# Batch 1's attention by pairs of heads: 64-row score products of two heads, and one split of q and k for each pair

## The chip, the cores and the metric

The kernel runs on one core of a Trainium2 chip. The metric is device time in microseconds (us) of one execution, the median of three runs. TensorE multiplies matrices, VectorE (DVE), ScalarE (ACT) and GpSimd (POOL) work on tiles in the on-chip memory, and DMA queues, most of them fed by SyncE (SP), carry data. An operand of TensorE has up to 128 rows; a product over 64 rows uses the lower or the upper half of them. One operand (the weights) is loaded by an instruction of its own, shown as PEld.

## The reference

Attention of two batches with eight heads each, 768 positions, 64 numbers a head. A query sees only the keys that fall into the same of 64 buckets. The result goes through two blocks of matrix products. The parts that this case touches are the scores:

```python
q_bits = (np.einsum('bhsd,dk->bhsk', q, proj) > 0)      # 6 bits
q_bucket = np.sum(q_bits * 2 ** np.arange(6), axis=-1)  # k the same
mask = q_bucket[:, :, :, None] == k_bucket[:, :, None, :]
scores = scale * np.matmul(q, k.transpose(0, 1, 3, 2))
scores = np.where(mask, scores, -1e9)
attn = np.exp(scores - max);  attn = attn / (sum + 1e-9)
x = np.matmul(attn, v)                    # then, per batch:
u = x + real(fft(fft(x, 1), 2));  un = layernorm(u)
x = u + relu(un @ w_ch1) @ w_ch2          # 512 -> 2048 -> 512
theta = x @ w_theta;  y = w_tok_r @ (x * cos) + w_tok_i @ (x * sin)
out = (x + y) + relu((x + y) @ w_ch)
```

All weights arrive as float64 and are split in the kernel into parts of which TensorE computes three products.

## The kernel before

**Stages.** Batch 0's attention runs first. Its Fourier products, layer norm and first block follow. Batch 1's attention is woven into that: its softmax work runs on VectorE, ScalarE and GpSimd while TensorE also works on batch 0's Fourier products and its two-layer MLP (names psm, unT, w1h, w1l, hh). Batch 1's Fourier products and MLP come next, and the last block of both batches ends the kernel.

**What sets the order.** The source gives each step a priority in microseconds (`at`, `sooner`), and a scheduler orders each engine's instructions by priority and by what its own cost model takes to be ready. So an engine's order isn't the order of the source. `tc.issue_after(x)` puts the instructions issued inside it behind instruction x, but only those on x's engine.

**Batch 1's attention.** Work goes by pairs of heads (j = 0 to 3); the q and k of a pair lie one head on rows 0 to 63, the other on rows 64 to 127 of a tile `tt`. `prep` (L265) builds for each head a float32r stack `stk` of 128 rows by four times 768: on one half of the rows the rounded q or k (ScalarE), on the other half a copy of it (DMA) or what rounding left of it (GpSimd), and in the rows that are left the bucket codes (TensorE products pss<-bits,pat and two ScalarE calls). `attn_S` (L331) makes a head's scores for 128 queries in four products of 128 rows by 384 columns, into one of three score buffers of the ring `PS` (L115, name pss). `attn_max` and `attn_exp` take the maximum on VectorE and the exponential on ScalarE, `attn_split` splits into float16 parts, a DMA transposes them, `attn_AV` multiplies with the values into an accumulator (pso), and `attn_norm` divides for one head at a time. `attention` (L409) runs over four pairs, two heads and six query tiles; `T["ps"]` says behind which tiles a next step of the next pair's `prep` is issued.

**Batch 0's attention** (`prep_pair` L230, `pair_S` L313, `attention_first`) already goes by pairs, with float32 products of 64 rows, and normalises with `pair_norm` for both heads of a pair.

**Float64 loads.** `from_f64` (L163) loads a chunk of 512 float64 numbers to one of `NCV` = 3 buffers (L161) and converts it with two ScalarE calls and one on VectorE.

Of the kernel before, what the change touches and what calls it, by code (L numbers as in the profile page):

```python
# [9 lines left out]
F32 = mybir.dt.float32  # L10
# [60 lines left out]
def fused_kernel(ctx, tc, A, out):  # L71
# [15 lines left out]
    def stt(eng, out, in0, in1, op, scale=1.0):  # L87
# [9 lines left out]
        ne=42, es=150, ld='ss', lc='s', ps=[[0, 3], [0, 5], [1, 0], [1, 5]])  # L97
# [45 lines left out]
    pat = mk(at_p, [128, 4, 128], BF16, "pat")  # L143
# [17 lines left out]
    CN, NCV = 512, 3  # L161
# [68 lines left out]
    def prep_pair(j, first=False):  # L230
# [19 lines left out]
        for qk in range(2):  # L250
            out = oh[:, qk].rearrange("p (a n) -> p a n", a=2)
            ps = PS("s")
            for g in range(2):
                mm(ps[:, g, 0:384], pat[64 * g:64 * g + 64, 2 + qk], bits[64 * g:64 * g + 64], True, True)
# [10 lines left out]
    def prep(b, j):  # L265

        tt = mk(at_p, [128, 2, S], F32, "tt")
        ld = {"s": SY, "a": AC, "p": PL}[T["ld"][b]]
        vr = mk(at_p, [128, 2 * NT * (D + 1)], F32, "vr")
        for o, i in ((tt[:, 0], A["qT"]), (tt[:, 1], A["kT"]), (vr, A["v"])):  # L270
            ld.dma_start(out=o, in_=i[b, j])
        pl_copy(tt[:, 1], tt[:, 1], 0.125)
        v2 = mk(vv_p, [128, 2, 2 * NT * (D + 1)], F16, "vv")

        def values():
            AC.activation(out=v2[:, 0], in_=vr, func=AF.Copy, scale=VS)
            stt(V, v2[:, 1], vr, v2[:, 0], ALU.subtract, VS)

        if j:
            values()  # L280
        yield
        st = []
        bits = mk(at_p, [64, 2, 384], BF16, "bits")
        ps = PS("s")
        into = [ps[:, g, 0:384] for g in range(2)]
        for g in range(2):
            for qk in range(2):
                mm(into[g][32 * qk:32 * qk + 32], projb, tt[:, qk, 384 * g:384 * g + 384], True, True)
        V.tensor_scalar(out=bits, in0=ps[0:64, :, 0:384], scalar1=0.0, scalar2=None, op0=ALU.is_gt)
        made[4 * b + j] = [st, v2.rearrange("p a (h k c) -> p a h k c", h=2, k=NT)]  # L290
        for h in range(2):
            yield
            dd, oo = half[h], half[1 - h]
            s = mk(st_p, [128, 4, S], F32R, "stk")
            st.append(s)
            AC.activation(out=s[dd, 0], in_=tt[dd, 0], func=AF.Copy)
            SY.dma_start(out=f(s[dd, 1]), in_=f(s[dd, 0]))
            stt(PL, s[oo, 1], tt[dd, 0], f(s[dd, 0]), ALU.subtract)
            AC.activation(out=s[dd, 2], in_=tt[dd, 1], func=AF.Copy)
            SY.dma_start(out=f(s[oo, 3]), in_=f(s[dd, 2]))  # L300
            stt(PL, s[dd, 3], tt[dd, 1], f(s[dd, 2]), ALU.subtract)
            pp = PS("s")
            for g in range(2):
                mm(pp[:, g, 0:384], pat[0:64, h], bits[:, g], True, True)
            for qk in range(2):
                i = half[h if qk else 1 - h]
                AC.activation(out=s[oo, 2 * qk].rearrange("p (a n) -> p a n", a=2), in_=pp[i, :, 0:384],
                              func=AF.Sign if qk else AF.Relu, bias=hb[i, qk:qk + 1])
            if not j and not h:
                values()  # L310
        yield
# [19 lines left out]
    def attn_S(st, t):  # L331
        ps = PS("s")
# [49 lines left out]
    def pair_norm(j, part, o, hi=None):  # L382
# [5 lines left out]
        x = x_t[0][:, 3 * part:3 * part + 3].rearrange("p t (a c) -> p t a c", a=2)[:, :, :, lo]  # L388
# [4 lines left out]

    def attn_norm(b, h, o):

        r = mk(sm_p, [128, NT, 1], F32, "r", bufs=2)
        V.tensor_scalar(out=r, in0=o[:, :, D:D + 1], scalar1=VS * 1e-9, scalar2=None, op0=ALU.add)
        V.reciprocal(out=r, in_=r)
        x = x_t[b][:, :, 64 * h:64 * h + 64]
        V.tensor_tensor(out=x, in0=o[:, :, 0:D], in1=r.to_broadcast([128, NT, D]), op=ALU.mult)  # L400
# [8 lines left out]
    def attention(b, t0, pace, lead, hi_eng, lo_eng, after=lambda b, j: None):  # L409
        x_t[b] = mk(x_p, [128, NT, DM], F32, "x")  # L410
        n, w = 0, soft["p2"][0].shape[1]
        for j in range(4):
            i = 4 * b + j
            if i not in made:
                at(t0 + pace * n - lead)
                with after_gate("p1" if b else None):
                    run(prep(b, j))
            st, vv = made[i]
            for hh in range(2):
                h = PO[j] + 4 * hh  # L420
                at(t0 + pace * n)
                o = PS("o")[:, 0:NT * (D + 1)].rearrange("p (t d) -> p t d", t=NT)
                for t in range(NT):
                    at(t0 + pace * n)
                    ps = attn_S(st[hh], t)
                    with after_gate(0 if b and n >= T["n1"] else "ln0" if b and n >= T["n0"] else None):
                        p, m = attn_exp(ps)
                    if not t % w:
                        p2 = soft_tile("p2")
                    with after_gate(0 if b and n >= T["n1"] else None):  # L430
                        attn_split(p, p2[:, t % w].bitcast(F16).rearrange("p (a n) -> p a n", a=2), hi_eng(n), lo_eng(n))
                    if t % w == w - 1:
                        pt, trans = transposed(p2)
                        for i in range(w):
                            attn_AV(o, pt[:, 12 * i:12 * i + 12], vv, hh, t - w + 1 + i)
                    n += 1
                    if j < 3 and [hh, t] in T["ps"]:
                        at(t0 + pace * n - lead)
                        if [hh, t] == T["ps"][0]:
                            new = prep(b, j + 1)  # L440
                        next(new)
                at(t0 + pace * n - 30)
                attn_norm(b, h, o)
            after(b, j)

    def attention_first(pace, after):
# [7 lines left out]
        def av(n):  # L454
# [5 lines left out]
            if i == NT - 1:  # L460
                hi = PS("m")[:, 0:384].rearrange("p (t a c) -> p t a c", t=3, a=2) if j == 3 and part else None
                pair_norm(j, part, o[0], hi)
# [488 lines left out]
    attention(1, T["b1"], T["pace1"], T["lead"], pick(h1), pick(l1))  # L951
# [131 lines left out]
def _constants():  # L1083
# [19 lines left out]
    pat = np.zeros((128, 4, 128), np.float32)  # L1103
    hb = np.zeros((128, 2), np.float32)
    for c in range(128):
        bits = [(c % 64 >> i) & 1 for i in range(6)]
        for head in range(2):
            qk = (c < 64) ^ head
            for i in range(6):
                pat[32 * qk + 6 * head + i, head, c] = (2 * bits[i] - 1) * (1 if qk else BIG)  # L1110
# [54 lines left out]
```

## Time and profile before

| what | us |
|---|---|
| median of three runs (741.94 to 745.8) | 742.81 |
| the profiled execution, its own time | 742.76 |
| its span in the trace | 741.0 |
| TensorE busy (weight loads apart: 508.2) | 665.2 (90%) |
| VectorE, ScalarE, GpSimd busy | 399.7, 376.5, 371.2 |

TensorE's instructions start in the program's order, and so do those of every other engine. Its busy share is 50 to 70% between 120 and 210 us and 90% or more from about 240 us on. A product's end in the trace is modelled, so what a product costs is read from the starts: the start of the next product minus its own, in a stretch without idle time. A row of the timeline joins products of one kind that stand behind each other; "xcount" is their number. A wait in brackets is the idle time ahead of the row, with what ended it.

### The profile page before, as it was taken

Reading aid. Unit: us, or ns where it says so; the run is one execution under the profiler, and the core shown is the slowest. Engines: PE = TensorE matmul, PEld = TensorE weight load, DVE = VectorE, ACT = ScalarE, POOL = GpSimd, SP = SyncE. Lnnn points to the kernel's source line nnn. Section 1 sums busy time; section 2 is a strip of 40 time slices with the busy share of each in tenths; the row PEclk is TensorE's granted clock in tenths of the full one; section 3 lists DMA queues with packets and bytes.
Section 4 is the critical chain, followed back from the end, with each engine's and each line's share of the span. In section 5 each row is a group of like instructions: output and inputs, shape, how many; then the busy total and the mean of one; then the engine's idle time right before and its main releaser. Section 6 shows DMA issues by size and latency. Waiting matters only on the chain.

```text
span 741.0 us, 13335 instructions
## 1 busy us (share of the span) xinstructions
PE 665.2 (90%) x5354; PEld 508.2 (69%) x5354; DVE 399.7 (54%) x649; ACT 376.5 (51%) x603; POOL 371.2 (50%) x312
## 2 busy tenths in 40 slices
PE   5898898477687998999999999999999899979997
PEld 2465565355676656776786685786675798979997
DVE  1567787886898555443386671354322456352222
ACT  2555564967997878663322161354226555571010
POOL 2787887697796887785550030233213246631000
PEclk9999999899679999999999999999999999999999
DMA  9897976378899997777760252010014411551202
GB/s 346 184 173 147 156 109 143 107 182 224 206 223 214 254 213 213 137 130 123 119 191 2 29 122 44 26 47 1 0 46 147 159 40 31 173 184 44 85 1 86
DMA packets 161438, 93.69 MB, mean 126 GB/s; under 512 B 137056, under 2 KB 147552, under 8 KB 161376
## 3 DMA queue, kind: packets, MB, share of 16 engines
q1 hardware_dynamic: 159440, 86.27, 50.7%
q0 software_dynamic: 1936, 6.57, 2.5%
q8 instruction: 42, 0.69, 0.4%
q14 instruction: 20, 0.16, 0.1%
HBM read 49.82 MB, written 6.29 MB: 76 GB/s over the span
## 4 chain that ended last, share of the span: by engine, by line
PE 39%; issue 11%; POOL 11%; DMA 10%; ACT 6%; DVE 5%; SPq 0%; POOLq 0%; DVEq 0%; ACTq 0%
PE psm L62 26%; PE psf L62 10%; DMA r<-in_wtok 4%; POOL w1l L62 3%; POOL p L62 3%; ACT r L62 2%; PE pss L62 2%; DMA x<-p 2%; PE pso L62 2%; POOL pt L62 1%; DMA r<-in_w 1%; ACT stk L62 1%; DVE r L62 1%; DVE fa L62 1%; DMA r<-in_wch 1%
## 5 line engine op out<-in xcount | busy, mean ns | idle before, releaser
L62 PE MATMUL psm<-unT,w1h 128*128 128x256 f16 x768 | 130.9, 274 | 1.0 <-DVE hl L62 0.6
L62 PE MATMUL psm<-unT,w1l 128*128 128x256 f16 x384 | 105.2, 274 | 0.0
L62 DVE SCALAR_TENSOR_TENSOR r<-r 128x512 uint32<-128x512 uint32 (+1 forms) x64 | 61.8, 969 | 75.6 <-ACT r L62 67.8
L62 PEld LDWEIGHTS <-w1h 128*128 128x128 f16 (+1 forms) x774 | 75.3, 99 | 17.4 <-issue 6.1
L62 POOL TENSOR_TENSOR w1l<-r,w1h 128x384 fp32r<-128x384 f32 (+1 forms) x36 | 41.1, 1154 | 58.9 <-ACT w1h L62 58.6
L62 PEld LDWEIGHTS <-hh 128*128 128x128 f16 x384 | 37.2, 98 | 45.0 <-issue 3.4
L62 ACT ACTIVATE r<-r,chalf 128x512 uint32<-128x512 uint32 (+1 forms) x64 | 46.1, 720 | 40.7 <-DMA r<-in_wtok 19.2
L62 PE MATMUL pss<-stk 128*128 128x384 f32 x192 | 49.8, 388 | 17.5 <-ACT p L62 10.0
L62 PE MATMUL psm<-w2h,hh 128*128 128x512 f16 x192 | 59.6, 379 | 1.6 <-DVE hl L62 1.6
L64 PE MATMUL pss<-stk 64*128 64x384 f32 (+1 forms) x288 | 55.2, 469 | 6.5 <-ACT p L64 3.2
L62 DVE TENSOR_REDUCE nm<-pss 128x1 f32<-128x768 f32 x48 | 45.1, 947 | 27.4 <-PE pss L62 27.3
L62 PE MATMUL psm<-w2l,hh 128*128 128x512 f16 x192 | 59.8, 379 | 0.0
L62 PE MATMUL psm<-w2h,hl 128*128 128x512 f16 x192 | 59.6, 379 | 0.0
L62 POOL TENSOR_TENSOR p<-p,p 128x768 f16<-128x768 f32 x32 | 54.6, 1713 | 5.2 <-ACT p L62 4.3
L62 ACT ACTIVATE p<-pss,nm 128x768 f32<-128x768 f32 x48 | 42.7, 893 | 26.3 <-DVE nm L62 24.2
L64 DVE TENSOR_REDUCE nm<-pss 128x1 f32<-128x768 f32 x48 | 43.6, 950 | 19.8 <-PE pss L64 19.7
L62 DVE SCALAR_TENSOR_TENSOR hl<-psm,hh 128x512 f16<-128x512 f32 x48 | 32.8, 687 | 36.1 <-ACT hh L62 36.0
L62 PEld LDWEIGHTS pss<-stk 128*128 128x128 f32 x192 | 35.1, 208 | 23.9 <-ACT p L62 13.2
L62 ACT ACTIVATE hh<-psm 128x512 f16<-128x512 f32 x48 | 28.2, 592 | 39.8 <-PE psm L62 39.6
L62 PEld LDWEIGHTS <-w1l 128*128 128x128 f16 x384 | 37.8, 98 | 5.7 <-issue 1.3
L62 POOL TENSOR_TENSOR stk<-tt,stk 64x768 fp32r<-64x768 f32 x16 | 31.4, 1962 | 16.2 <-issue 12.9
L62 ACT ACTIVATE r<-r 128x512 f32<-128x512 f32 (+1 forms) x64 | 39.4, 615 | 0.0
(318 smaller groups left out, 1548.5 us busy)
## 6 DMA issues: line engine op xcount, KB each, us to landing
r<-in_w SPq DMA_DIRECT2D x32, 512.0 KB, 4.5
r<-in_wtok SPq DMA_DIRECT2D x24, 384.0 KB, 3.8
vr<-in_v SPq DMA_DIRECT2D x8, 390.0 KB, 3.5
stk<-stk SPq DMA_DIRECT2D x16, 192.0 KB, 3.2
xT<-xs SPq DMA_DIRECT2D x12, 256.0 KB, 2.6
xt<-xT SPq DMA_DIRECT2D x4, 768.0 KB, 5.0
out<-xt SPq DMA_DIRECT2D x8, 384.0 KB, 2.5
ct<-in_ct POOLq DMA_DIRECT2D x4, 579.0 KB, 7.7
```

Of the source, the lines that this page charges most:

```text
L62: return fn(*a, **k)
L64: self.last = fn(*a, **k)
```

## The change

Batch 1's attention goes by pairs like batch 0's.

- `prep(j)` splits q and k once for a pair, in calls of 128 rows: rounded parts by ScalarE, rest of q by GpSimd, rest of k by VectorE. There are no copies by DMA. The bucket codes lie in a bf16 tile `oh` of both heads.
- `split_S` makes the scores of both heads for one query tile in 16 products of 64 rows: four of the codes and twelve of the parts (hi·hi, hi·lo, lo·hi, over two column halves), written with the heads in turn. It takes two of the three score buffers.
- In the loop, `split_S` is issued inside `issue_after` of both exponentials of the last pair. The two heads' softmax follows, and the norm comes for three query tiles of both heads.
- `prep`'s steps are issued behind query tiles 1, 3 and 5, two at a time.
- `NCV` goes from 3 to 4, the code pattern `pat` from four blocks to two, and the area for GpSimd's DMA descriptors is 4096 bytes.

```diff
-    CN, NCV = 512, 3
+    CN, NCV = 512, 4
...
-    def prep(b, j):
+    def prep(j):
+        i = 4 + j
+        sp = mk(st_p, [128, 4, S], F32R, "stk")
+        tt, hi, lo = mk(at_p, [128, 2, S], F32, "tt"), sp[:, 0:2], sp[:, 2:4]
+        oh = mk(st_p, [128, 2, S], BF16, "oh")
...
+        AC.activation(out=hi[:, 0], in_=tt[:, 0], func=AF.Copy)
+        stt(PL, lo[:, 0], tt[:, 0], f(hi[:, 0]), ALU.subtract)
+        AC.activation(out=hi[:, 1], in_=tt[:, 1], func=AF.Copy, scale=0.125)
+        stt(V, lo[:, 1], tt[:, 1], f(hi[:, 1]), ALU.subtract, 0.125)
+        yield
...
-        for h in range(2):
-            yield
-            dd, oo = half[h], half[1 - h]
-            s = mk(st_p, [128, 4, S], F32R, "stk")
-            st.append(s)
-            AC.activation(out=s[dd, 0], in_=tt[dd, 0], func=AF.Copy)
-            SY.dma_start(out=f(s[dd, 1]), in_=f(s[dd, 0]))
-            stt(PL, s[oo, 1], tt[dd, 0], f(s[dd, 0]), ALU.subtract)
-            AC.activation(out=s[dd, 2], in_=tt[dd, 1], func=AF.Copy)
-            SY.dma_start(out=f(s[oo, 3]), in_=f(s[dd, 2]))
-            stt(PL, s[dd, 3], tt[dd, 1], f(s[dd, 2]), ALU.subtract)
...
-    def attn_S(st, t):
-        ps = PS("s")
+    def split_S(i, t):
+        x, oh = made[i][:2]
+        ps = [PS("s") for h in range(2)][::-1]
         c = slice(128 * t, 128 * t + 128)
-        for k in range(2):
+        pairs = [(oh, oh)] + [(x[a], x[k]) for a, k in P3]
+        for n, (q, k) in enumerate(pairs):
             for g in range(2):
-                mm(ps[:, g, 0:384], st[:, k, c], st[:, 2 + k, 384 * g:384 * g + 384], k == 0, k == 1)
+                for h in (1, 0):
+                    mm(ps[h][:, g, 0:384], q[half[h], 0, c], k[half[h], 1, 384 * g:384 * g + 384], n == 0, n == 3)
         return ps
...
+            both = ExitStack()
+            for e in last:
+                both.enter_context(tc.issue_after(e.ins))
+            with both:
+                ps = split_S(4 + j, t)
...
-                attn_norm(b, h, o)
+                pair_norm(1, j, t // 3, o)
...
-    nc = _bacc.Bacc("TRN2", target_bir_lowering=False, num_devices=1)
+    nc = _bacc.Bacc("TRN2", target_bir_lowering=False, num_devices=1, dynamic_dma_scratch_size=4096)
```

Three places in the built programs show what moves. The first is TensorE where batch 1's scores begin. `pss` are score buffers, `psm<-ct,hlz2` the first Fourier products. Before:

```order
L62 MATMUL pss_2438<-bits_2410,pat_89 128x384
L62 MATMUL pss_2444<-stk_2417 128x384 x4
L62 MATMUL pss_2473<-stk_2417 128x384 x4
L62 MATMUL pss_2502<-stk_2417 128x384 x4
L62 MATMUL pss_2531<-stk_2417 128x384 x4
L62 MATMUL psm_1987<-ct_160,hlz2_171 128x386 x9
```

After, from the last two of the first pair's products to the last of the second pair's, which the same Fourier products follow:

```order
L62 MATMUL pss_2433<-stk_2403 128x384
L62 MATMUL pss_2434<-stk_2403 128x384
L62 LDWEIGHTS oh_2405
L62 MATMUL pss_2499<-oh_2405 128x384
L62 LDWEIGHTS oh_2405
L62 MATMUL pss_2499<-oh_2405 128x384
L62 MATMUL pss_2499<-stk_2403 128x384 x6
L62 LDWEIGHTS oh_2405
L62 MATMUL pss_2500<-oh_2405 128x384
L62 LDWEIGHTS oh_2405
L62 MATMUL pss_2500<-oh_2405 128x384
L62 MATMUL pss_2500<-stk_2403 128x384 x6
```

The first pair (2433 and 2434) stands in turn, the second (2499 and 2500) one head behind the other. Four head tiles stand ahead of the Fourier products in both.

The second place is TensorE among batch 0's MLP products (`psm<-unT`). Before, a head's score products there:

```order
L62 MATMUL pso_3036<-vv_2566,x_118 128x65
L62 MATMUL pss_3365<-stk_3066 128x384 x4
L62 LDWEIGHTS w1l_1890
L62 MATMUL psm_4342<-unT_2197,w1l_1890 128x256
L62 LDWEIGHTS w1h_1889
L62 MATMUL psm_4342<-unT_2197,w1h_1889 128x256
```

After, a head's eight products of 64 rows:

```order
L62 MATMUL psm_4490<-unT_2197,w1h_1889 128x256
L62 LDWEIGHTS oh_3002
L62 MATMUL pss_3369<-oh_3002 128x384
L62 LDWEIGHTS oh_3002
L62 MATMUL pss_3369<-oh_3002 128x384
L62 MATMUL pss_3369<-stk_3000 128x384 x6
L62 LDWEIGHTS w1l_1890
L62 MATMUL psm_4490<-unT_2197,w1l_1890 128x256
```

Here one head (buffer 3369) stands alone between MLP products, and the other head of its pair comes later. Of the 24 pairs 9 stand in turn, 12 one head behind the other, and 3 partly in turn.

The third place is VectorE ahead of the Fourier products: `fa` is the fold of x with which they begin, `hlz2` and `hle` are the operands, `nm` the score maxima, `r64` float64 chunks. Before:

```order
L62 SCALAR_TENSOR_TENSOR r64_1905<-r64_1905 128x512
L62 TENSOR_REDUCE nm_2449<-pss_2444 128x1
L62 TENSOR_TENSOR fa_158<-x_175,psm_1861 128x6x64 x2
L62 SCALAR_TENSOR_TENSOR vv_2566<-vr_2561,vv_2566 128x780
L62 TENSOR_REDUCE nm_2478<-pss_2473 128x1
L62 TENSOR_TENSOR psm_1869<-fa_158 128x384
L62 TENSOR_TENSOR fa_158<-fa_158 128x6x64
L62 TENSOR_TENSOR psm_1872<-fa_158,psm_1869 128x384
L62 TENSOR_TENSOR psm_1876<-fa_158 128x260
L62 TENSOR_REDUCE nm_2507<-pss_2502 128x1
L62 TENSOR_TENSOR hlz2_171<-psm_1872,hlz2_171 128x6x64
L62 TENSOR_TENSOR hle_172<-psm_1876,hle_172 128x4x65
```

After:

```order
L62 TENSOR_TENSOR fa_158<-x_175,psm_1861 128x6x64 x2
L62 SCALAR_TENSOR_TENSOR stk_2565<-tt_2566,stk_2565 128x768
L62 TENSOR_TENSOR psm_1869<-fa_158 128x384
L62 TENSOR_TENSOR fa_158<-fa_158 128x6x64
L62 SCALAR_TENSOR_TENSOR vv_2860<-vr_2568,vv_2860 128x780
L62 TENSOR_TENSOR psm_1872<-fa_158,psm_1869 128x384
L62 TENSOR_TENSOR psm_1876<-fa_158 128x260
L62 SCALAR_TENSOR_TENSOR r64_1919<-r64_1919 128x512
L62 TENSOR_REDUCE nm_2451<-pss_2433 128x1
L62 TENSOR_REDUCE nm_2475<-pss_2434 128x1
L62 SCALAR_TENSOR_TENSOR r64_1926<-r64_1926 128x512
L62 TENSOR_TENSOR hlz2_171<-psm_1872,hlz2_171 128x6x64
```

The maxima move behind the fold, and the rest of the second pair's k (stk_2565) and a float64 chunk stand between the fold and the operands.

## Rows read from the trace of the kernel before

**Rows 1.** Busy time by stage; columns: us, five engines' busy us (count), clock, DMA, GB/s.
```profile
135.70:210.90 75.20, 49.13 (x360) 38.54 (x358) 61.14 (x96) 63.57 (x104) 61.31 (x44) 0.79 0.78 194
210.90:372.00 161.10, 148.75 (x1501) 108.96 (x1501) 88.81 (x125) 107.12 (x150) 116.94 (x81) 0.99 0.86 179
540.00:741.00 201.00, 188.88 (x1055) 170.42 (x1052) 73.75 (x116) 75.39 (x141) 56.73 (x52) 0.98 0.29 91
```

**Rows 2.** TensorE's waits from 120 to 385 us: us in total, times, longest.
```profile
PE pss L62 <- ACT p L62: 13.1, 8, 2.9
PE pss L62 <- ACT stk L62: 7.4, 3, 5.8
```

**Rows 3.** TensorE's timeline at 304 us: start, length, instruction, count.
```profile
304.33 0.94 PE L62 MATMUL pss<-stk 128*128 128x384 f32 x4
305.11 0.28 PE L62 MATMUL psm<-unT,w1l 128*128 128x256 f16 x1
```

**Rows 4.** The chain of waits from 715 us on: start, us, what.
```profile
720.08 16.66 PE psf L62 x96
```

**Rows 5.** TensorE's timeline at three places with products of 64 rows.
```profile
135.70 0.82 PE L62 MATMUL pss<-bits,pat 64*128 64x384 bf16 x4
...
56.87 0.34 PE L64 MATMUL pss<-bits,pat 64*128 64x384 bf16 x2
57.14 0.33 PE L64 MATMUL psm<-ident,pt 128*128 128x128 f32 x1
...
49.16 1.88 PE L64 MATMUL pss<-stk 64*128 64x384 f32 x11
```

**Rows 6.** Lengths by tile: smallest, mean, largest ns; from and to in us.
```profile
L62 PE MATMUL pss<-bits,pat x20: 322/333/524, 11.1 to 320.2; 64*128 64x384 bf16 x20
L64 PE MATMUL pss<-stk x288: 319/482/1005, 13.4 to 122.5; 64*128 64x384 f32 x88, 64*128 64x384 bf16 x56
```

**Rows 7.** Weight loads, 40 to 60 us: busy us, mean ns, idle before.
```profile
L64 PEld LDWEIGHTS pss<-stk 64*128 64x128 f32 x40 | 3.8, 186 | 2.5 <-ACT w1l L64 0.6 <-ACT pt L64 0.4 <-ACT p L64 0.2
```

**Rows 8.** Groups of the preparation, 120 to 380 us, shapes apart.
```profile
L62 POOL TENSOR_TENSOR stk<-tt,stk 64x768 fp32r<-64x768 f32 x16 | 31.4, 1962 | 16.2 <-issue 12.9 <-ACT stk L62 2.4
L62 ACT ACTIVATE stk<-pss,hb 64x768 fp32r<-64x768 f32 x16 | 14.3, 896 | 0.3
L62 ACT ACTIVATE stk<-tt 64x768 fp32r<-64x768 f32 x16 | 12.6, 833 | 2.6 <-PE pss L62 2.6
L62 DVE SCALAR_TENSOR_TENSOR vv<-vr,vv 128x780 f16<-128x780 f32 x4 | 5.1, 1263 | 0.8 <-ACT vv L62 0.8
L62 POOL TENSOR_SCALAR tt<-tt 128x768 f32<-128x768 f32 x4 | 4.4, 1099 | 0.0
```

**Rows 9.** Timelines of TensorE, then VectorE and ScalarE, from 142 to 205 us.
```profile
142.34 1.65 PE L62 MATMUL pss<-stk 128*128 128x384 f32 x4 [5.82 <-ACT stk L62]
...
153.29 1.84 PE L62 MATMUL psm<-ct,hlz 128*128 128x386 f32 x9 [1.96 <-DVE hle L62]
...
188.58 1.11 PE L62 MATMUL psm<-ident,un 128*128 128x128 f32 x4 [1.10 <-DVE un L64]
...
203.46 1.65 PE L62 MATMUL pss<-stk 128*128 128x384 f32 x4 [2.03 <-ACT p L62]
...
144.90 1.01 DVE L62 TENSOR_TENSOR fa<-x,psm 128x384 f32<-128x384 f32 x2
...
144.14 0.49 ACT L64 ACTIVATE x<-psm 128x384 f32<-128x384 f32 x1
```

**Rows 10.** Busy time and clock of a stretch behind idle time; columns as in rows 1.
```profile
142.50:148.00 5.50, 3.14 (x8) 2.12 (x8) 4.75 (x6) 5.41 (x9) 3.43 (x4) 0.50 0.42 143
```

**Rows 11.** TensorE's waits from 500 to 741 us.
```profile
PE psf L62 <- ACT xh L62: 3.6, 3, 2.2
PE psm L62 <- ACT w1h L62: 2.4, 1, 2.4
```

**Rows 12.** ScalarE's timeline at 584 us.
```profile
584.54 0.78 ACT L62 ACTIVATE r<-r,chalf 128x512 uint32<-128x512 uint32 x1 [4.08 <-DMA r<-in_wch]
```

More of the change, by code (lines that the diff above doesn't have):

```diff
@@ L263, in prep_pair @@
         made[j].append(v2.rearrange("p a (h k c) -> p a h k c", h=2, k=NT))
-    def prep(b, j):
-        tt = mk(at_p, [128, 2, S], F32, "tt")
-        ld = {"s": SY, "a": AC, "p": PL}[T["ld"][b]]
-        vr = mk(at_p, [128, 2 * NT * (D + 1)], F32, "vr")
[L270 to L280, printed above, removed]
-        yield
-        st = []
-        bits = mk(at_p, [64, 2, 384], BF16, "bits")
-        ps = PS("s")
-        into = [ps[:, g, 0:384] for g in range(2)]
+    def prep(j):
[3 more added lines that the diff above has]
+        oh = mk(st_p, [128, 2, S], BF16, "oh")
+        vr = mk(at_p, [128, 2 * NT * (D + 1)], F32, "vr")
+        for o, a in ((tt[:, 0], A["qT"]), (tt[:, 1], A["kT"]), (vr, A["v"])):
+            SY.dma_start(out=o, in_=a[1, j])
+        made[i] = [(hi, lo), oh]
+        yield
+        AC.activation(out=hi[:, 0], in_=tt[:, 0], func=AF.Copy)
[3 more added lines that the diff above has]
+        yield
+        bits = mk(at_p, [128, 384], BF16, "bits")
+        ps = PS("s")[:, 0, 0:384]
@@ L311, in prep @@
-        yield
+                c = 64 * g + 32 * qk
+                mm(ps[c:c + 32], projb, tt[:, qk, 384 * g:384 * g + 384], True, True)
+        V.tensor_scalar(out=bits, in0=ps, scalar1=0.0, scalar2=None, op0=ALU.is_gt)
+        yield
+        for qk in range(2):
+            ps = PS("s")
+            for g in range(2):
+                mm(ps[:, g, 0:384], pat[64 * g:64 * g + 64, qk], bits[64 * g:64 * g + 64], True, True)
+            AC.activation(out=oh[:, qk].rearrange("p (a n) -> p a n", a=2), in_=ps[:, :, 0:384],
+                          func=AF.Sign if qk else AF.Relu, bias=hb[:, qk:qk + 1])
+            yield
@@ L313, in pair_S @@
+        v2 = mk(vv_p, [128, 2, 2 * NT * (D + 1)], F16, "vv")
+        AC.activation(out=v2[:, 0], in_=vr, func=AF.Copy, scale=VS)
+        stt(V, v2[:, 1], vr, v2[:, 0], ALU.subtract, VS)
+        made[i].append(v2.rearrange("p a (h k c) -> p a h k c", h=2, k=NT))
     def pair_S(j, t):
@@ L407, in after_gate @@
         return es
[L409 to L414, printed above, removed]
-                at(t0 + pace * n - lead)
[L416 to L441, printed above, removed]
@@ new lines, in attention @@
+    def attention(t0, pace, lead, hi_eng, lo_eng):
+        x_t[1] = mk(x_p, [128, NT, DM], F32, "x")
+        at(t0 - lead)
+        with after_gate("p1"):
+            run(prep(0))
+        last = []
+        for s in range(4 * NT):
+            j, t = s // NT, s % NT
+            n = 2 * s
+            at(t0 + pace * n)
+            if not t % 3:
+                o = PS("o")[:, 0:NT * (D + 1)].rearrange("p (t d) -> p t d", t=NT)
+            both = ExitStack()
[3 more added lines that the diff above has]
+                ps = split_S(4 + j, t)
+            last = []
+            for hh in (1, 0):
+                with after_gate(0 if n >= T["n1"] else "ln0" if n >= T["n0"] else None):
+                    p, m = attn_exp(ps[hh])
+                last.append(m[1])
+                p2 = soft_tile("p2")
+                with after_gate(0 if n >= T["n1"] else None):
+                    attn_split(p, p2[:, 0].bitcast(F16).rearrange("p (a n) -> p a n", a=2), hi_eng(n), lo_eng(n))
+                pt, trans = transposed(p2)
+                attn_AV(o, pt, made[4 + j][2], hh, 2 * (t % 3) + hh)
+                n += 1
+            if j < 3 and t in T["ps"]:
+                at(t0 + pace * n - lead)
+                if t == T["ps"][0]:
+                    new = prep(j + 1)
+                run(take(new, 2))
+            if t % 3 == 2:
```

42 lines of the change are left out of this document (9 added, 33 removed).

## The prediction

> **What bounds the kernel now.** I read the table of stages first, then the waits of TensorE, then single places of its timeline, then the groups of the preparation, and last the waits of the end. The span is 741.0 us, the profiled execution's own time 742.76 us, and the median of the three timed runs 742.81 us, so a sum made against this execution needs no correction.
>
> The stages [rows 1] show where time can be won. From 135.7 to 210.9 us, between the end of batch 0's attention and the first product of the first MLP, TensorE is busy 49.13 of 75.20 us: 26.1 us idle, at a mean granted clock of 0.79. From 210.9 to 372 us, where batch 1's attention runs between the MLP's products, it is busy 148.75 of 161.10 us: 12.4 us idle. In the last stage 12.1 us are idle. TensorE's instructions keep their order, so the end comes at the sum of its work and of its idle time. In batch 1's attention the longest of these waits are those of the score products for the exponentials, 13.1 us, and for the operands made by ScalarE, 7.4 us [rows 2].
>
> **The scores, step by step.** A head and a query tile now take four products of 128 rows. They stand at 304.33, and the next product starts at 305.11: 0.78 us, or 1.56 us for two heads [rows 3]. The same kind of product, 128 rows by 384 columns with a weight load each, runs at 16.66/96 = 0.174 us in the last 17 us of the kernel [rows 4].
>
> The change makes 16 products of 64 rows of the two heads: four of the bucket codes (bf16) and twelve of q and k. Whether two of them, on the two halves of the rows, run side by side is the question. Four bf16 products on one half of the rows took 0.82 us, and two that stand on different halves took 0.34 us, as long as one alone [rows 5, 6]. On one half the step is then (0.82-0.33)/3 = 0.163 us, and on two halves the second product is free. Eleven of batch 0's float32 passes, in turn over both halves, took 1.88 us of which 0.48 is the last one's length, so 0.14 us a step, less than the 0.186 us of the weight load that each has [rows 5 to 7]: loads run side by side as well.
>
> So a pair in turn costs 8 steps of about 0.19 us, 1.5 us. If nothing overlapped it would be 4 x 0.163 + 12 x 0.174 = 2.7 us; if all did, 8 x 0.163 = 1.3 us. I take 1.5, near the float32 row. A pair whose heads stand one behind the other costs the 2.7 us. Going between 64 and 128 rows costs about 0.1 us each way: the bf16 pair at 56.87 is followed by a 128-row product at 57.14, 0.27 us later instead of 0.163 [rows 5]. That makes 1.7 us for a pair in turn, 2.9 us for one head behind the other, against 1.56 now.
>
> The order of the built program decides, and it isn't the one that the source writes. The edges put behind the last pair's exponentials are edges on ScalarE; the products are on TensorE, so they hold nothing there, and the scheduler moves a head's products forward when its score buffer is free first. Of the 24 pairs 9 stand in turn, 12 head behind head, and 3 in part. From the first MLP product on there are 18.5 pairs: 8.5 head behind head (25 us), 7 in turn (12 us), 3 in part (about 2.3 us each, 7 us), together 44 us, where 36 head tiles took 28 us. **This step: +16 us of TensorE work** (+4 if grouped products overlap as well, +23 if turns do not help at all).
>
> Would the engine itself take the second head's products forward? No row shows it, because no two groups on different halves stand behind each other in this trace. The Trainium skill, page "TensorE: Matmul & The Clock Gate", section "The mechanism", says products keep the program's order in start and end, and only weight loads are taken forward. By that rule the grouped pairs stay at 2.9 us and the sum stands; without it, it would be the first rival below.
>
> **The preparation.** GpSimd loses 16 subtractions of 64 rows (31.4 us) and four scalings (4.4 us) and gets four subtractions of 128 rows, about 1.9 us each by the 64-row group: about 28 us less. ScalarE loses 32 calls (12.6 + 14.3 us) and gets 16 of the same lengths, 13 us less. VectorE gets four calls like the 1.26 us of the value split, 5 us. Sixteen copies of 192 KB leave the DMA queue [rows 8]. All of this lies beside TensorE's work from 142 to 320 us. It counts only where it ends one of the 12.4 us of idle time, and more TensorE work ahead of a wait shortens that wait too. Against it stands a new tie: both score buffers now belong to one pair, so TensorE can't write the next pair's scores while this one's are reduced, and waits like the 13.1 us for exponentials can grow. From all idle time of the stage gone (-12) to half as many waits again for exponentials (+7), I take **-5 us**.
>
> **The start of batch 1's attention.** The first scores start at 142.34 behind ScalarE's four code tiles, the Fourier products at 153.29, the transposes of the first normalised rows at 188.58, the first MLP product at 210.9 [rows 1, 9]. The Fourier chain begins with VectorE's fold at 144.90, which follows ScalarE's copy of x at 144.14 [rows 9]. In the new order ScalarE has still about as much ahead of that copy (four float64 chunks instead of three, and the second pair's parts, in place of six of the eight stk calls), so the fold stays. Then VectorE has the second pair's k part (1.26 us), a float64 chunk and two maxima ahead of the split that the Fourier products at 153.29 wait for [rows 9], and TensorE has the second pair, head behind head, ahead of the Fourier products. Behind it fewer head tiles (11, not 12) stand ahead of the first MLP product. TensorE's clock was at 1.2 GHz, half of its upper level, in the stretch behind the idle time before 142 us [rows 10], when four score products took 1.65 us instead of 0.94 [rows 3, 9]; the second pair can fall into such a stretch. Between 7 us gained (two head tiles with their waits for exponentials, 1.65 + 2.03 us each by the one at 203.46 [rows 9]) and 10 us lost (second pair and Fourier products at the lower level), I take **+2 us**.
>
> **The fourth buffer for float64 chunks.** In the last stage TensorE waits 3.6 us for xh and 2.4 us for w1h [rows 11]. Both come from ScalarE standing behind a load: one call waited 4.08 us for w_ch, with xh behind it [rows 12]. A fourth chunk lets a load start earlier. The w1h wait should go, and with it the clock's fall behind it; the new order still has two w_ch loads ahead of the second xh, so that wait stays in part. Between -8 (both waits and their stretches at the lower clock) and +1 I take **-4 us**. The smaller descriptor area costs nothing that I can see: GpSimd's seven loads of a batch have the same order and nothing waits on it.
>
> **Sum:** +16 - 5 + 2 - 4 = +9, so **752 us**.
>
> **Rivals.**
> 1. *Grouped heads overlap as well.* The two halves run side by side also when the program lists head behind head; 8.5 pairs cost 1.2 us less, 10 us in all: 742 us. For it: both 0.34 and 0.14 us show the halves are independent. Against: an in-order queue would need to look past eight products.
> 2. *Faster: the freed engines give back the idle time.* GpSimd and ScalarE are 73 and 67% busy from 210.9 to 372 [rows 1], DMA 0.86. With 28 and 13 us less there, the waits of that stage all go (-12), the first MLP product starts 7 us earlier, the end wins 8: 743 + 16 - 12 - 7 - 8 = 732 us. It decides if the waits that GpSimd's splits and transposing DMAs set go by more than the scores add; as the scores may also be some us cheaper, I hold 728 to 739 under this.
> 3. *Slower still: turns do not help for float32r, and the Fourier chain loses its 10 us.* Each weight load of 0.186 us is taken alone, so all pairs cost 2.9 us: 752 + 7 x 1.2 + 8 = 768 us.
> 4. *The wait is not what it says.* If the hardware's queue did hold each pair behind both exponentials with TensorE idle, each of 18 pairs would pay a maximum and an exponential; MLP products stand between nearly all pairs in the order, so this is only in the upper bound of the second step.
>
> **Chances.** Forecast 0.45 (745 to 760 us), first rival 0.13, second 0.24, third and fourth 0.18. A measurement of this kernel tells about 0.5% (3.7 us) from no change. The forecast gives nearly all of its chance to slower; the first rival lies mostly within; the second is faster. Slower 0.59, same 0.16, faster 0.25. The range that holds 8 in 10 takes in part of the second rival and most of the third: 734 to 766 us; the forecast's own is 745 to 760.
>
> **What would show it.** In the new profile: groups of eight 64-row products of one head with starts 0.16 to 0.175 us apart, and turns with two starts in 0.19 us. TensorE's busy time from the first MLP product to the last value product should rise by about 11 us and its idle time fall. The Fourier products should start at 156 to 161 us, the first MLP product at 209 to 218. The w1h wait should be gone at the end. I am wrong if grouped products overlap, if the stage's idle time goes nearly to nothing, or if the first MLP product comes before 205 us.

## The result and the profile after

The changed kernel takes 752.69 us (median of ten runs, 746.14 to 757.47), the kernel before 742.11 us beside it: a ratio of 1.011, interval 1.007 to 1.0149. A second set of five runs gave 749.23 us, ratio 1.0088, interval 1.0055 to 1.012. The change makes the kernel slower by 1%, as forecast. The ten runs lie in two groups, four at 746 us (mean granted clock 0.956 to 0.963) and six at 753 us and above (0.941 to 0.956), so their median falls into the upper group, and the ratio on record, which leaves the slowest run out, is below the 1.014 of the two medians.

The rows below are of the second profile of the changed kernel, span 749.5 us. The first profile puts the first MLP product at 219.1 us instead of 217.4 and takes 536.6 us behind it instead of 532.1, so two executions of one program differ by some us in a stage. Each stage below is read from one execution, and small differences between stages are to be taken with that in mind.

One correction to the text on the kernel before and on the change: in batch 1's attention the ring of score buffers has two, not three. The third is given back when batch 0's attention ends (`third.release()` in the kernel). The prediction counts with two.

**By stage.** The stages are cut at TensorE's own landmarks: batch 1's first score product, the first MLP product, batch 1's first Fourier product, the first product of the last block, the end. Columns are those of [rows 1]: length, then busy us and count of TensorE, its weight loads, VectorE, ScalarE and GpSimd, then granted clock, DMA share and GB/s. The last line is all that stands behind the first MLP product. Before:

```profile
142.34:210.90 68.56, 48.31 (x353) 38.25 (x354) 55.81 (x90) 57.02 (x94) 54.84 (x42) 0.77 0.80 197
210.90:396.83 185.93, 173.00 (x1688) 126.01 (x1688) 110.87 (x162) 112.91 (x162) 128.20 (x99) 0.99 0.80 173
396.83:571.19 174.36, 173.99 (x1137) 121.68 (x1135) 74.91 (x156) 67.35 (x124) 37.16 (x37) 1.00 0.20 46
571.19:741.00 169.81, 157.69 (x863) 151.56 (x861) 66.93 (x105) 61.36 (x115) 47.72 (x43) 0.97 0.28 91
210.90:741.00 530.10, 504.69 (x3682) 399.25 (x3681) 252.71 (x423) 241.62 (x398) 213.08 (x179) 0.99 0.44 105
```

After:

```profile
142.46:217.41 74.95, 54.10 (x373) 45.55 (x373) 57.94 (x90) 55.19 (x94) 51.20 (x40) 0.69 0.75 196
217.41:415.31 197.90, 188.78 (x1859) 134.65 (x1858) 108.30 (x162) 101.37 (x146) 110.88 (x87) 0.98 0.70 141
415.31:589.60 174.29, 174.29 (x1139) 121.89 (x1137) 77.29 (x160) 68.67 (x127) 37.63 (x38) 1.00 0.19 50
589.60:749.50 159.90, 153.71 (x863) 148.86 (x861) 63.04 (x102) 57.45 (x108) 46.18 (x42) 1.00 0.28 88
217.41:749.50 532.09, 516.79 (x3854) 405.40 (x3853) 248.63 (x423) 227.49 (x381) 194.69 (x167) 0.99 0.41 95
```

The start costs 6.5 us (the first MLP product at 217.41, not 210.90), the attention among MLP products 12.0 us, the middle nothing; the last stage gives 9.9 us back. That makes the 8.5 us between the spans. In the attention stage TensorE has 15.8 us more to do and is idle for 9.1 us, not 12.9. At the start its idle time is nearly the same, 20.8 us against 20.2: there too it is the work that grew.

**The scores.** Summed by starts with idle time taken out, score products take 61.0 us in all after and 44.7 us before, 16.3 us more. From the first MLP product on it is 41.5 against 28.8 us, and ahead of it 19.5 against 15.9 us. TensorE's timeline shows both kinds of pairs; columns as in [rows 3]:

```profile
241.06 0.49 PE L62 MATMUL pss<-oh 64*128 64x384 bf16 x2
241.26 1.34 PE L62 MATMUL pss<-stk 64*128 64x384 f32 x6
242.54 0.28 PE L62 MATMUL psm<-unT,w1h 128*128 128x256 f16 x1
...
298.21 0.50 PE L62 MATMUL pss<-oh 64*128 64x384 bf16 x4
298.41 1.36 PE L62 MATMUL pss<-stk 64*128 64x384 f32 x12
299.70 0.28 PE L62 MATMUL psm<-unT,w1l 128*128 128x256 f16 x1
```

One head alone, eight products, takes 242.54 - 241.06 = 1.48 us. A pair in turn, sixteen products, takes 299.70 - 298.21 = 1.49 us. Two heads before took 1.56 us [rows 3].

**The waits** of TensorE, as in [rows 2, 11], up to 416 us and behind it:

```profile
PE pss L62 <- ACT p L62: 14.9, 3, 8.2
PE pss L62 <- ACT oh L62: 6.6, 2, 5.6
...
PE psf L62 <- ACT xh L62: 2.0, 2, 1.6
```

Three waits for exponentials take 14.9 us, where eight took 13.1; one of the three, 8.2 us, lies at the start. The wait for w1h at the end is gone; that for xh is 2.0 instead of 3.6 us.

**The start.** VectorE's timeline answers to the second part of [rows 9]:

```profile
143.37 1.02 DVE L62 TENSOR_TENSOR fa<-x,psm 128x384 f32<-128x384 f32 x2 [3.08 <-ACT x L64]
144.30 1.16 DVE L62 SCALAR_TENSOR_TENSOR stk<-tt,stk 128x768 fp32r<-128x768 f32 x1
...
147.66 1.61 DVE L62 SCALAR_TENSOR_TENSOR vv<-vr,vv 128x780 f16<-128x780 f32 x1
...
150.22 1.36 DVE L62 SCALAR_TENSOR_TENSOR r<-r 128x512 uint32<-128x512 uint32 x1
151.51 1.81 DVE L62 TENSOR_REDUCE nm<-pss 128x1 f32<-128x768 f32 x2
```

And TensorE's, to the first part:

```profile
142.46 0.82 PE L62 MATMUL pss<-oh 64*128 64x384 bf16 x4 [5.56 <-ACT oh L62]
142.81 2.40 PE L62 MATMUL pss<-stk 64*128 64x384 f32 x12
153.44 0.80 PE L62 MATMUL pss<-oh 64*128 64x384 bf16 x2 [8.23 <-ACT p L62]
...
157.35 2.94 PE L62 MATMUL psm<-ct,hlz 128*128 128x386 f32 x8
```

The first pair's scores are done at 145.2, but their maxima stand behind two splits and a float64 chunk and come at 151.51. TensorE waits 8.23 us where it waited 2.19 us before, and the second pair's products run at a granted clock of 0.50, which is 1.2 GHz. So do the Fourier products behind them: eight recorded ones take 2.94 us where nine took 1.84 at a granted clock of 1.00 [rows 9].

```profile
157.35:160.29 2.94, 2.94 (x10) 2.75 (x9) 2.94 (x1) 0.00 (x0) 2.94 (x3) 0.50 0.95 314
```

Is the long wait the cause of the lower clock? Two other traces speak against it. The kernel before with the fourth buffer alone (experiment 1) has no such wait, and its Fourier products are as slow:

```profile
154.77 3.26 PE L62 MATMUL psm<-ct,hlz 128*128 128x386 f32 x9 [2.68 <-DVE hle L62]
```

With all pairs in turn (experiment 2) the wait is as long, and nine take 2.26 us:

```profile
153.71 0.48 PE L64 MATMUL pss<-oh 64*128 64x384 bf16 x1 [8.24 <-ACT p L62]
...
157.22 2.26 PE L62 MATMUL psm<-ct,hlz 128*128 128x386 f32 x9
```

Summed as the scores were, the Fourier products of the start take 24.8 us against 20.8 before, 4.0 us more, and the score products 3.6 us more; smaller groups take 1.8 us less and idle time is 0.6 us more. That is the 6.4 us by which the stage is longer. The traced execution of the kernel before had a mean granted clock of 0.969, which three of 56 later runs of it reach, so a part of the 4.0 us may be that execution's own.

### The profile page after: what moved, and what is told of

Same layout as the page of the kernel before. It is cut to its first block, busy times and chain, and to the rows that moved or that the text cites. A ratio compares the mean times of both kernels' runs of the same rounds, so it can differ in the third digit from the quotient of the medians.

```text
span 755.7 us, 13650 instructions
## 1 busy us (share of the span) xinstructions
PE 688.3 (91%) x5546; PEld 525.8 (70%) x5546; DVE 398.1 (53%) x653; ACT 361.7 (48%) x587; POOL 342.6 (45%) x296
## 4 chain that ended last, share of the span: by engine, by line
PE 41%; POOL 11%; issue 11%; DMA 9%; DVE 6%; ACT 5%; SPq 0%; POOLq 0%; ACTq 0%; DVEq 0%
PE psm L62 27%; PE psf L62 10%; POOL p L62 4%; POOL w1l L62 3%; PE pss L62 3%; DMA r<-in_w 2%; DMA pt<-pt 2%; ACT r L62 2%; DMA pt<-p 2%; POOL pt L62 1%; DMA x<-p 1%; DMA r<-in_wtok 1%; PE pso L62 1%; DVE fa L62 1%; DVE psm L62 1%
## 5 line engine op out<-in xcount | busy, mean ns | idle before, releaser
L62 DVE SCALAR_TENSOR_TENSOR r<-r 128x512 uint32<-128x512 uint32 (+1 forms) x64 | 53.0, 834 | 50.5 <-ACT r L62 45.0
L62 PE MATMUL pss<-stk 64*128 64x384 f32 x288 | 55.6, 399 | 0.0
L62 PEld LDWEIGHTS pss<-stk 64*128 64x128 f32 x288 | 44.5, 215 | 2.6 <-issue 1.0
L62 PE MATMUL pss<-oh 64*128 64x384 bf16 x96 | 22.7, 365 | 21.8 <-ACT p L62 14.4
```

The source lines that it names most:

```text
L62: return fn(*a, **k)
```

## The experiments

All times stand beside runs of the kernel before on the same chip.

**1. The changed kernel again, and a two by two.** `after_again` is the changed kernel; `before_ncv4` is the kernel before with the fourth buffer and the smaller descriptor area of the change (the area was not tried apart, and counts to the buffer here); `after_ncv3` is the change with three buffers:

```diff
-    CN, NCV = 512, 3
+    CN, NCV = 512, 4
...
-    nc = _bacc.Bacc("TRN2", target_bir_lowering=False, num_devices=1)
+    nc = _bacc.Bacc("TRN2", target_bir_lowering=False, num_devices=1, dynamic_dma_scratch_size=4096)
```

```diff
-    CN, NCV = 512, 4
+    CN, NCV = 512, 3
```

> The changed kernel once more, for a profile beside the one of 757.5 us, whose TensorE clock was at 1.2 GHz for 91 us against 49 us of before. Ten runs so far lie in two groups, 746.1 to 746.5 and 752.7 to 753.8 us. Theory A (the terms add up: scores and the late start cost, the end gives back): 746 to 754 us, the first MLP product 4 to 8 us later than before, scores behind it 12 us longer, the last stage 6 to 9 us shorter, and the two groups differ by stretches at the lower clock of some 15 us. Rival B (the clock alone): if this execution has no more time at the lower clock than before, it ends at 742 us.

> The kernel before with four buffers for float64 chunks and the small descriptor area, and nothing else. Theory A: the wait for w1h of 2.4 us and one of the waits for xh go, with the stretches at the lower clock behind them; the last stage is 4 to 9 us shorter, 733 to 738 us. Rival: the end got shorter in the changed kernel because its attention stage is longer and loads have more time ahead of it; then 742 us and the last stage is as before.

> The changed kernel with three buffers for float64 chunks. Theory A: the last stage loses its 6 to 9 us, 756 to 761 us. Rival (the buffers do not matter at the end): 752 us. The order of the scores changes a little with it (1 or 2 pairs more in turn), worth about 1 to 2 us.

| us | three buffers | four buffers | ratio of the new column to before (interval) |
|---|---|---|---|
| scores and preparation of before | 741.79 | 739.29 | 0.9959 (0.9935 to 0.9982) |
| scores and preparation of the change | 762.63 | 749.23 | 1.0088 (1.0055 to 1.012); three buffers 1.0265 (1.0232 to 1.0297) |

The buffer alone brings 2.5 us, under the change 13.4; the rest of the change costs 20.8 us without it and 9.9 with it. `after_again` came as theory A says, with a last stage shorter by 9.9 us instead of 6 to 9. `before_ncv4` has the shorter end (6.8 us), but misses 733 to 738 us: its start is later by 4.9 us, which theory A had not, and the stretch between is 2.1 us longer. `after_ncv3` loses 6.7 us in the last stage as expected, and more ahead of it, so it lies above its 756 to 761 us. Start, last stage and all behind the first MLP product, of the buffer alone:

```profile
142.93:215.84 72.91, 54.95 (x375) 45.83 (x376) 55.10 (x80) 58.57 (x97) 56.72 (x43) 0.69 0.80 199
...
578.23:741.20 162.97, 154.28 (x863) 148.83 (x861) 65.05 (x102) 57.42 (x108) 46.32 (x42) 1.00 0.28 87
215.84:741.20 525.36, 503.93 (x3660) 398.01 (x3659) 250.77 (x432) 237.29 (x393) 207.33 (x177) 0.99 0.42 103
```

and of the change without it:

```profile
140.76:213.21 72.45, 50.54 (x382) 43.07 (x381) 55.83 (x90) 50.38 (x86) 45.88 (x37) 0.71 0.68 175
...
592.80:759.40 166.60, 154.88 (x863) 148.84 (x861) 66.48 (x105) 61.85 (x115) 48.63 (x43) 1.00 0.29 93
213.21:759.40 546.19, 514.55 (x3846) 404.07 (x3845) 250.90 (x424) 235.74 (x390) 196.45 (x170) 0.99 0.39 98
```

The fourth buffer moves the first MLP product by +4.9 us (215.84 against 210.90) in the one and +4.2 us (217.41 against 213.21) in the other; the change itself moves it by 2.3 and 1.6 us. Behind that product the buffer gives 4.7 us in the one and 14.1 us in the other, of which 6.7 are the last stage and 7.4 lie ahead of it. Those 7.4 us come although the scores are dearer with four buffers: the built order has 13 pairs in turn with three buffers and 9 with four, and score products take 52.6 us in all against 61.0 (the expectation had 1 or 2 us). What four buffers save there is idle time: with three, TensorE is idle for 19.9 us from the first MLP product to the last stage, with four for 9.1.

What the buffer changes can be seen in ScalarE's waits for loads of w_tok from 136 us on, total, times, longest. Before:

```profile
ACT r L62 <- DMA r<-in_wtok: 19.2, 12, 3.1
```

With the buffer alone:

```profile
ACT r L62 <- DMA r<-in_wtok: 12.8, 10, 3.1
```

The change with three:

```profile
ACT r L62 <- DMA r<-in_wtok: 21.3, 17, 3.2
```

The change with four:

```profile
ACT r L62 <- DMA r<-in_wtok: 12.6, 10, 2.6
```

With the loads of w added (11.5, 8.4, 14.6 and 8.4 us) ScalarE waits 30.7, 21.2, 35.9 and 21.0 us: the buffer takes 9.5 us away in the one and 14.9 in the other. The waits for w_ch, which the prediction named, don't shrink: 6.8, 9.0, 7.3 and 8.2 us. ScalarE's order holds exponentials behind such loads; by which of them TensorE's idle time falls was not traced.

**2. All pairs in turn, and all head behind head.** `turn` chains the 16 products of a pair on TensorE in the order written; `group` also puts the loop over heads outside.

```diff
+        PE.hold, PE.last = True, None
         for n, (q, k) in enumerate(pairs):
...
+        PE.hold = False
```

```diff
+        PE.hold, PE.last = True, None
-        for n, (q, k) in enumerate(pairs):
-            for g in range(2):
-                for h in (1, 0):
+        for h in (1, 0):
+            for n, (q, k) in enumerate(pairs):
+                for g in range(2):
...
+        PE.hold = False
```

> The changed kernel with the 16 products of each pair chained on TensorE in the order of the source, so that all 24 pairs stand in turn. Theory A: from the first MLP product on, scores cost 18 to 19 pairs of 1.5 us, about 28 us instead of 41 us, so 13 us less of TensorE's work; waits grow by less, 738 to 746 us. Rival (the tie of both buffers): a pair can't start until both heads of the last one have their exponentials, TensorE's idle time grows by 13 us or more, 752 us or above.

> The changed kernel with all 24 pairs chained head behind head. Theory A after the run with all pairs in turn (772 us, where 10 us less of products met 25 us more of idle time): the freedom of a head to start when its own buffer is free is worth more than the turns. Scores cost 24 pairs of about 2.85 us, 68 us in all instead of 61 us, waits fall by 0 to 5 us: 747 to 756 us. Rival (any chain on TensorE costs, turns do not matter): 765 us or more.

In turn: 772.52 us, ratio 1.0396 (1.0368 to 1.0424). Head behind head: 757.2 us, 1.02 (1.0168 to 1.0231). Start and all behind the first MLP product, in turn:

```profile
142.72:213.17 70.45, 46.23 (x367) 39.14 (x366) 55.95 (x86) 51.02 (x87) 48.55 (x38) 0.74 0.75 188
...
213.17:769.90 556.73, 516.57 (x3861) 401.64 (x3860) 254.10 (x428) 231.78 (x386) 196.99 (x169) 0.97 0.39 94
```

and head behind head:

```profile
143.50:226.97 83.47, 67.62 (x487) 56.81 (x486) 67.47 (x115) 62.91 (x104) 62.12 (x47) 0.70 0.77 195
...
226.97:756.30 529.33, 515.18 (x3740) 404.72 (x3739) 240.71 (x399) 221.32 (x370) 181.81 (x160) 1.00 0.38 93
```

Turns make the products cheap, 44.2 us in all (group 73.3, the change 61.0), and the start is 4.2 us earlier. Yet behind the first MLP product it is 24.6 us longer than the change, with TensorE idle for 40 us, not 15. Its waits there:

```profile
PE psm L62 <- DMA unT<-u: 9.0, 1, 9.0
PE psf L62 <- issue: 8.4, 1, 8.4
```

Both lie between 420 and 480 us, behind the attention: its last value product is at 410.5 us, 17 us later than in the change, so batch 0's MLP runs out before batch 1's Fourier operands are there (8.4 us), and later TensorE waits for the first normalised rows of batch 1 (9.0 us). The rival holds in its size, but not as a wait of the scores: from the first MLP product to 410 us TensorE waits for no exponential, and the order that is built sets MLP products in that place and ends the attention late. `group`, with a chain as long but heads free of each other, has no such wait, and its last value product is at 381.4 us, so the chain alone doesn't cost this. That leaves the prediction's "new tie", a pair in turn that needs both buffers at once; a run with a third buffer, which would show it directly, was not made. `group` lies just above its range.

**3. The added products alone.** `half` leaves hi·lo and lo·hi out of the scores.

```diff
-        pairs = [(oh, oh)] + [(x[a], x[k]) for a, k in P3]
+        pairs = [(oh, oh), (x[0], x[0])]
```

> The changed kernel with the products hi·lo and lo·hi left out of the scores (8 products of 64 rows for a pair instead of 16, so the scores are rounded); preparation, norms and buffers stay. It takes the cost of the added products away alone: head behind head a pair then costs about 1.5 us, as a pair of 128-row tiles did. Theory A (TensorE's work is what counts): scores from the first MLP product on fall from 41.5 to about 22 us and before it by 8 us, and 725 to 732 us come out. Rival (the chain of the softmax and the two score buffers set the pace): idle time takes the place of the products, 740 us or more.

729.19 us, ratio 0.9814 (0.9797 to 0.983), as theory A has it. Start and all behind the first MLP product:

```profile
143.04:213.19 70.15, 52.04 (x372) 41.65 (x371) 53.28 (x78) 52.26 (x90) 49.40 (x38) 0.62 0.78 193
...
213.19:728.30 515.11, 500.96 (x3665) 388.26 (x3663) 250.52 (x436) 229.22 (x385) 195.14 (x168) 0.99 0.41 101
```

Score products fall by 24.8 us (36.2 in all) and the time by 20.0 us against 749.23: four fifths of that work are on the path. Against the kernel before with the same buffers (739.29) it is 10.1 us faster, with 9.2 us less of score products (36.2 against 45.4). So the cheaper preparation, 28 us less on GpSimd and 13 on ScalarE by the prediction's count, is worth no more than about 1 us net of what the ties cost, and that is within what runs of one kernel differ by.

**4. The first pair ahead of the chunks.** `early` writes the first pair before the fifth float64 chunk and puts the later chunks and splits behind its maxima.

```diff
...
-        timed(take(cw1, T["k0"]), T["w1"], T["w1s"])
+        timed(take(cw1, T["e0"]), T["w1"], T["w1s"])
+    second = attention(T["b1"], T["pace1"], T["lead"], pick(h1), pick(l1))
+    next(second)
+    gate["nmg"] = gate["nm"][:2]
+    with after_gate("cv"), after_gate("nmg"):
+        timed(take(cw1, T["k0"] - T["e0"]), T["w1"] + T["e0"] * T["w1s"], T["w1s"])
...
```

> The changed kernel with its first pair written ahead of the fifth float64 chunk, and the chunks and the second pair's splits on VectorE put behind the first pair's maxima. Nothing else on any engine is taken away. Theory A (the late start comes from VectorE's order, which puts two chunks and two splits between the fold and the maxima and Fourier operands, and from the lower clock behind TensorE's wait): Fourier products at 150 to 153 us instead of 157, the first MLP product 4 to 8 us earlier, 209 to 214 us, end 741 to 746 us. Rival (ScalarE's fourth chunk or the 64-row products are what delays it): the first MLP product stays at 216 us or later and the end at 749 us.

757.23 us, ratio 1.0191 (1.0161 to 1.0221); neither theory gives that. TensorE's first Fourier products, and the two stretches:

```profile
149.82 3.26 PE L62 MATMUL psm<-ct,hlz 128*128 128x386 f32 x9 [4.13 <-DVE hle L62]
```

```profile
142.95:214.49 71.54, 53.85 (x402) 45.28 (x401) 54.65 (x85) 53.33 (x91) 51.02 (x40) 0.71 0.79 194
...
214.49:757.50 543.01, 519.17 (x3826) 405.63 (x3825) 252.84 (x429) 228.97 (x383) 192.81 (x167) 0.98 0.39 95
```

The Fourier products come 7.5 us earlier, so VectorE's order did delay them. But they still run at the lower clock (nine take 3.26 us, at a granted clock of 0.50), the first MLP product comes only 2.9 us earlier, and behind it 10.9 us are lost. The new order moves instructions in the whole attention; which of them loses the time was not tried.

**5. Towards a faster kernel.** All on the kernel before: five buffers; four buffers with 8 instead of 12 chunks ahead of the first layer norm (`k0=8`); five with the chunks behind the third held behind the first pair's codes on ScalarE; the same also behind ScalarE's last copy of x. The last two add, after the first three chunks:

```diff
...
+    at(T["b1"] - T["lead"])
+    with after_gate("p1"):
+        run(prep(1, 0))
+    gate["codes"] = made["code", 1, 0, 1]
+    with after_gate("cv"), after_gate("codes"):
+        timed(take(cw1, T["k0"] - T["e0"]), T["w1"] + T["e0"] * T["w1s"], T["w1s"])
...
```

> The kernel before with five buffers for float64 chunks. Theory (a buffer takes ScalarE's waits for loads away at the end and gives back a part at the start, where more chunks come ahead of the scores): ScalarE's waits for w and w_tok loads fall below the 21.2 us that four buffers left, the first MLP product comes at 216 to 221 us, and 736 to 742 us come out. Rival (the loads are as early as they can be with four): waits and time as with four, 739 us.

> The kernel before with four buffers, and 8 instead of 12 of the first MLP's 16 weight chunks converted ahead of batch 0's first layer norm. Theory (chunks on ScalarE and VectorE delay batch 1's first scores and the Fourier operands): the first MLP product at 208 to 213 us instead of 216, and 732 to 737 us. Rival (the first chunks are the same ones, and the last four now come late for the first MLP): 739 us or more.

> The kernel before with five buffers, of which only three chunks may run on ScalarE ahead of the bucket codes of batch 1's first pair; the others stand behind them. Theory (a buffer wins behind the first MLP product, 14 us with five, and what it loses lies in the first scores, which started at 150.5 us instead of 142.3): first scores at 141 to 143 us, the first MLP product at 211 to 217 us, the part behind it 512 to 517 us as with five buffers, 726 to 734 us. Rival (the late start and the short part behind it are one thing: what starts later finds its operands ready): the part behind it goes back to 521 us or more, 737 us or above.

> The same with the fourth and fifth chunk also behind ScalarE's copy of batch 0's last x, with which the Fourier chain begins. Theory: besides the first scores, the Fourier products come 1 to 2 us earlier than without, and the first MLP product with them: 209 to 214 us, 725 to 733 us. Rival: chunks put off here are missing later, the part behind the first MLP product grows by what the start wins, and the time stays as in the run beside it.

| kernel | us | ratio (interval) | first MLP product at |
|---|---|---|---|
| five buffers | 739.11 | 0.9952 (0.9917 to 0.9987) | 228.57 |
| four, eight chunks first | 744.8 | 1.0031 (0.9995 to 1.0067) | 222.21 |
| five, chunks behind the codes | 745.68 | 1.0061 (1.0032 to 1.009) | 218.34 |
| five, also behind the copy of x | 739.52 | 0.995 (0.9915 to 0.9985) | 222.63 |

Five buffers:

```profile
150.51:228.57 78.06, 55.20 (x375) 46.14 (x375) 53.84 (x84) 58.55 (x97) 56.62 (x43) 0.70 0.75 182
...
228.57:744.40 515.83, 499.63 (x3660) 395.94 (x3659) 252.92 (x426) 235.53 (x391) 210.56 (x177) 0.99 0.42 104
```

Five, also behind the copy of x:

```profile
142.19:222.63 80.44, 55.13 (x397) 45.68 (x398) 59.43 (x90) 65.95 (x108) 62.60 (x47) 0.69 0.80 194
...
222.63:738.50 515.87, 499.96 (x3643) 395.89 (x3639) 245.68 (x424) 230.69 (x384) 203.74 (x174) 0.99 0.42 102
```

Five buffers take 14 us off behind the first MLP product and put 18 on ahead of it; the execution that was traced took 746 us where the median is 739.11, so a part of the 18 is its own. ScalarE's waits for w and w_tok fall to 15.6 us, as expected, but the first MLP product is later than the 216 to 221 us given. With eight chunks first it is at 222 us instead of 208 to 213, and the time is that of the rival. With the chunks held back the first scores stand at 140.7 and 142.2 us again instead of 150.5, as expected, but the first MLP product stays late and neither run reaches its 725 to 734 us: the theory of the start is refuted there, and what sets it is open. Four buffers alone, five, and five with both holds beat both kernels, by 0.4 to 0.5%; they don't differ from each other.

## Why the prediction came true, and where its terms were off

| term | forecast | measured |
|---|---|---|
| scores from the first MLP product on | +16 (+4 to +23) | +12.7 (41.5 - 28.8) |
| preparation, idle time of that stage | -5 (-12 to +7) | -3.8 (9.1 - 12.9), not the preparation's alone |
| start | +2 (-7 to +10) | +6.5 |
| fourth buffer, last stage | -4 (-8 to +1) | -9.9, of which the buffer 6.7 to 6.8 |
| sum | +9 | +8.5, with 3.0 of small terms: value products +2.4, second-layer products +2.5 (a part of them at the lower clock), code products -1.8 |

**The scores: right.** A pair in turn was put at 1.5 us and took 1.49; one head behind the other at 2.9 and took 2 x 1.48. The order decided, as forecast. The Trainium skill ("TensorE: Matmul & The Clock Gate", section "The mechanism") says that only weight loads are taken forward past products; the trace agrees: products of one head alone start about 0.17 us apart (eight in 1.48 us, the step to the next MLP product included) and no second head overlaps. So rival 1 fell. All score products from the first MLP product on came to 41.5 us where the prediction summed 44, so the term is 3 us too high.

**The tie: right in direction, its mechanism in part argued.** `turn` shows what ties in all pairs go with: 24.6 us more behind the first MLP product. They come as a late end of the attention and not as longer waits for exponentials, which is how the prediction had it. In the change 12 of 24 pairs are free of it.

**The preparation: small, as forecast, but the agreement is not shown to be its own.** `half` leaves it about 1 us at most, net of the ties. The -3.8 us of idle time stand only with the fourth buffer: with three, the same stage of the changed kernel is idle for 17.0 us, 4.0 more than before. The prediction gave the buffer no part there. Rival 2, in which the freed engines give idle time back, fell with `half`.

**The start: the step that was mis-sized.** The text says ScalarE has about as much ahead of its copy of x, so the fold stays. The fold did stay (143.37 against 144.90). It also named what VectorE has ahead of the Fourier operands. What it missed by the sums of the start is work of TensorE: 3.6 us more of score products and 4.0 us more of Fourier products, these at the lower clock, which the prediction had only as a possibility in its upper bound. It also missed that the first pair's own maxima stand behind VectorE's work, but idle time in all is 0.6 us more, so that wait alone is not the cost. Of 6.5 us, 4.2 to 4.9 go with the fourth buffer by the two by two, to which the prediction gave only a gain at the end. Why the first MLP product comes later with it stays open, as in experiment 5.

**The fourth buffer: right in sign, too small.** The bound of -8 counted only the waits that TensorE shows at the end and their stretches at the lower clock. By the two by two 6.7 to 6.8 us of the 9.9 come with the buffer; the other 3.2 come with the rest of the change (169.81 against 166.60 us with three buffers), and nothing here says how. In the changed kernel the buffer is worth another 7.4 us ahead of the last stage, which no row of before could show: there the same stretch is 2.1 us longer with it.

**Rival 3**, at 768, needed turns that don't help; they do. **Rival 4**: the block that puts a pair behind both exponentials changes no engine's order; the program built without it reads the same, row for row. The waits for exponentials are those of score buffers.

The two misses, +4.5 at the start and -5.9 at the end, cancel, and that is luck; that the first median is 752.69 us and not the second set's 749.23 is luck as well. The forecast of 752 us is better than its terms.

## What to carry to other kernels

Products on two halves of the rows cost half only if the order that is built has them side by side, and putting them side by side ties their outputs: count pairs in the built order, then count buffers. A part of a change that looks like a side matter (one more load buffer) can be the larger gain; a two by two shows it, and shows that its price falls elsewhere. A sum that comes out right isn't proof of its terms; compare stage by stage.

## What the runs showed of the hardware

Sixteen score products of 64 rows with the halves in turn took 1.49 us, eight on one half 1.48 us: a second product on the other half was nearly free, and since twelve of the sixteen have float32r operands and four bf16, this holds for both.

What the clock costs a short stage can be read from one kind of product: nine Fourier products took 1.84 us at a granted clock of 1.00 (2.4 GHz) in the kernel before, and 3.26 us at 0.50 (1.2 GHz) in `early`. Behind a wait of 8.2 us they ran at the lower level in the change and partly at the upper one in `turn`; which it is isn't settled by the length of that one wait.
